# GroupNorm over 32 groups: the unrolled passes of VectorE and TensorE become small loops with the buffer number in a register

## Chip, cores and metric

The kernel runs on one NeuronCore of a Trainium2 chip; nothing else is placed on the chip by it. The metric is the device time of one execution in microseconds (us). The kernel before takes 633.19 us, the median of three runs (632.77 to 633.47).

## What is computed

The input is a bfloat16 tensor of 128 samples, 1024 channels and 32 x 16 points. Each sample's channels are split into 32 groups of 32; a group's 16384 values are brought to mean 0 and variance 1, and each channel is then scaled and shifted.

```python
G = 32
B, C, H, W = x.shape            # 128, 1024, 32, 16, bfloat16
xr = x.reshape(B, G, C // G, H, W)
mu = xr.mean(axis=(2, 3, 4), keepdims=True)
var = ((xr - mu) ** 2).mean(axis=(2, 3, 4), keepdims=True)
xn = (xr - mu) / jnp.sqrt(var + 1e-5)
return xn.reshape(B, C, H, W) * g[None, :, None, None] + b[None, :, None, None]
```

## The kernel before

A tile holds four samples: partition p carries one (sample, group) pair, and along the partition lie that group's 32 channels of 512 points, 32 KB. There are 32 tiles of 4 MB, each loaded once and stored once, and six buffers `xt[0..5]` in SBUF that tiles use in turn (tile i uses buffer (i + 4) mod 6).

Four engines handle each tile in a chain:

- **SyncE** (`sync_program`) issues every transfer, on one queue, in an order written out in the code. The first six loads go out at once. Then for each tile it waits for VectorE's count `s_dve` and issues the store (L171). After the stores of tiles 1, 4, 7, ... 25 it issues the next loads (two after tile 1, otherwise three; L163); each first waits until the store that empties its buffer has landed. Behind the six first loads and behind each run of loads it issues one *spacer* (L157), a load of 64 bytes a partition into a tile that nobody reads. There are ten of these.
- **TensorE** (`tensor_program`) waits for the load (L192) and sums the tile along the partition: 32 matmuls of 512 columns with the identity as weights, all added up in one PSUM bank `pa[j]` (L194). All 32 stand in the program for each of the six buffers.
- **VectorE** (`vector_program`) reduces the 512 columns of that bank to the negative mean (`mean`, L211). This mean of tile j+1 stands in the program ahead of the scaling of tile j.
- **ScalarE** (`scalar_program`) sums (x - mean) squared over the tile in two halves (L316), then makes the standard deviation with two small operations (L330, L337).
- **VectorE** then takes the reciprocal (L223), makes 32 scales and 32 shifts per partition (L226, L233), and runs 32 instructions of 512 points, one per channel, in place over the tile (L243). The last one raises `s_dve`.

VectorE, TensorE and ScalarE each run a counted loop (`loop`), a trip of which handles six tiles: the body is the six steps written out, every address a constant. It is split in two parts (`first`: buffers 0 to 3, `second`: 4 and 5) and entered at the second, because 32 tiles are not a multiple of six. For VectorE and TensorE the option `ahead` puts the set-up code behind the loop body. At the end of a trip each engine lowers the semaphores that it counts with (`settle` and `counts`), which costs VectorE three semaphore instructions, one register addition and a branch every six tiles.

## Time and profile before

| | |
|---|---|
| median of three runs | 633.19 us |
| profiled execution, its own time | 633.13 us |
| its span, first to last instruction | 631.3 us |
| busy: ScalarE | 476.2 us (75%) |
| busy: VectorE | 375.8 us (60%) |
| busy: TensorE matmul | 255.1 us (40%) |
| transfers: 32 loads, 32 stores of 4096 KB, 10 spacers of 8 KB | 268.57 MB, mean 425 GB/s |
| mean granted TensorE clock | 0.73 |

The profile's times are of the one profiled execution. The span runs from the first to the last instruction, and the execution's own time is 1.83 us longer. "Busy" counts engine work only; register, branch and semaphore instructions are not in it. The queue of an engine name with a q (SPq) stands for its issuing of transfers. "PEq L192" as a releaser is TensorE's wait for a load.

### The profile page before, as it was taken

To read this page: it belongs to the slowest core of one execution; us is meant where nothing else is said; L and a number is where in the kernel's file an instruction comes from. 1 tells how busy PE (TensorE), PEld (TensorE's weight loads), DVE (VectorE), ACT (ScalarE), POOL (GpSimd) and SP (SyncE) were. 2 spreads that over 40 slices of the span, in tenths; PEclk is the share of its full clock that TensorE was granted. 3 is DMA by queue.
4 is the path that set the end of the run, shared out by engine and by line. 5 is a ranking of instruction groups with operands and counts; after the bars stand their busy time and mean duration, and the time that the engine had idled before them with its cause. 6 is when DMAs were issued, how large, how long until landed. Compare 5 with 4: busy or idle time off the path is not lost. (4 is left out here: it accounts for less than half of the span.)

```text
span 631.3 us, 3704 instructions
## 1 busy us (share of the span) xinstructions
PE 255.1 (40%) x1009; PEld 105.4 (17%) x1025; DVE 375.8 (60%) x1188; ACT 476.2 (75%) x194; POOL 0.9 (0%) x7
## 2 busy tenths in 40 slices
PE   0967409009602750582087018404720770095000
PEld 0423103003201320230032003101300230032000
DVE  0057777774772777077727735770777177447771
ACT  0499999995994699189929965993899199649930
POOL 0000000000000000000000000000000000000000
PEclk9998858658855985687578659855975796598555
DMA  8999999999999999999999999999999999999996
GB/s 363 432 432 414 434 432 432 438 432 432 430 432 434 430 430 434 432 430 432 432 432 432 432 432 430 432 432 432 430 432 434 432 430 432 432 432 436 438 394 283
DMA packets 10756, 268.57 MB, mean 425 GB/s; under 512 B 2560, under 2 KB 2560, under 8 KB 2560
## 3 DMA queue, kind: packets, MB, share of 16 engines
q1 hardware_dynamic: 10656, 268.52, 99.0%
q10 hardware_dynamic: 96, 0.00, 0.0%
q14 instruction: 3, 0.02, 0.0%
q8 instruction: 1, 0.02, 0.0%
HBM read 134.30 MB, written 134.22 MB: 425 GB/s over the span
## 5 line engine op out<-in xcount | busy, mean ns | idle before, releaser
L316 ACT ACTIVATE ja<-xt,negmean 128x8192 fp8e5<-128x8192 bf16 x64 | 455.5, 7117 | 126.9 <-DVE jd L211 125.5
L194 PE MATMUL pa<-xt,eye 128*128 128x512 bf16 x1008 | 254.9, 414 | 312.4 <-PEq L192 310.9
L243 DVE TENSOR_SCALAR xt<-xt,scl,bia 128x512 bf16<-128x512 bf16 x1024 | 333.7, 408 | 1.2
L194 PEld LDWEIGHTS pa<-xt,eye 128*128 128x128 bf16 x1024 | 105.3, 105 | 461.6 <-issue 366.0
L211 DVE TENSOR_SCALAR_CACHE_REDUCE jd<-pa 128x512 bf16<-128x512 f32 x33 | 22.7, 687 | 147.3 <-PE pa L194 145.4
L223 DVE RECIPROCAL rstd<-std 128x1 f32<-128x1 f32 x32 | 5.2, 163 | 78.1 <-ACT std L337 78.1
L316 ACT ACTIVATION_READ_ACCUMULATOR ja<-xt,negmean 128x1 f32 x64 | 11.9, 186 | 0.0
L337 ACT ACTIVATE std<-sq,half 128x1 f32<-128x1 f32 x32 | 9.4, 295 | 1.0
L330 ACT ACTIVATE half<-sq,eps_t 128x1 f32<-128x1 f32 x32 | 8.9, 278 | 0.0
L233 DVE SCALAR_TENSOR_TENSOR bia<-scl,negmean,gb 128x32 f32<-128x32 f32 x32 | 8.1, 252 | 1.1
L226 DVE TENSOR_SCALAR scl<-gb,rstd 128x32 f32<-128x32 f32 x32 | 7.7, 241 | 1.1
L262 DVE COPY gb<-gb_p 128x64 f32<-128x64 f32 x1 | 0.2, 226 | 10.7 <-PE gb_p L181 10.7
L181 PE MATMUL gb_p<-gb_b,rep 32*128 32x64 bf16 x1 | 0.2, 231 | 12.5 <-DMA gb_b<-in_b_dram 12.5
L211 DVE DVE_READ_ACCUMULATOR jd<-pa 128x1 f32 x33 | 2.7, 83 | 0.0
L312 ACT ACT_TABLE_LOAD x1 | 1.3, 1283 | 1.9 <-issue 1.9
L181 PEld LDWEIGHTS gb_p<-gb_b,rep 32*128 32x128 bf16 x1 | 0.1, 100 | 12.5 <-DMA gb_b<-in_b_dram 12.5
L261 DVE MEMSET ones_b<- 128x128 bf16 x1 | 0.2, 165 | 1.9 <-issue 1.9
L289 POOL TENSOR_SCALAR_AFFINE_SELECT rep<-ones_b 32x128 bf16<-32x128 bf16 x1 | 0.3, 303 | 0.0
L280 POOL TENSOR_SCALAR_AFFINE_SELECT eye<-ones_b 128x128 bf16<-128x128 bf16 x1 | 0.3, 294 | 1.7 <-DVE ones_b L261 1.7
L312 ACT ACTIVATE warm<-eps_t 128x1 f32<-128x1 f32 x1 | 0.2, 203 | 0.0
L298 POOL TENSOR_SCALAR eps_t<-ones_b 128x1 f32<-128x1 bf16 x1 | 0.2, 205 | 0.0
L378 POOL MEMSET const-uint8-127<- 128x1 uint8 x1 | 0.1, 103 | 0.0
(3 smaller groups left out, 0.3 us busy)
## 6 DMA issues: line engine op xcount, KB each, us to landing
xt<-in_x_dram SPq DMA_DIRECT2D x32, 4096.0 KB, 29.1
out_dram<-xt SPq DMA_DIRECT2D x32, 4096.0 KB, 33.2
spare<-in_x_dram SPq DMA_DIRECT2D x10, 8.0 KB, 29.2
gb_b<-in_g_dram ACTq DMA_DIRECT2D x1, 2.0 KB, 7.8
gb_b<-in_b_dram ACTq DMA_DIRECT2D x1, 2.0 KB, 11.0
```

The costliest lines, as they stand in the source:

```text
L181: pe.matmul(out=gb_p[:].rearrange("p a k -> p (a k)"), lhsT=rep[:], rhs=gb_b[:].rearrange("q a k -> q (a k)"), start=True, stop=True,).the ...
L194: m = pe.matmul(out=pa[j][:], lhsT=eye[:], rhs=xt[j][:, k * MM_FREE : (k + 1) * MM_FREE], start=(k == 0), stop=(k == NMM - 1),)
L211: dve.tensor_scalar(out=jd[j % 2][:], in0=pa[j % NBUF][:], scalar1=-inv_n, scalar2=None, op0=ALU.mult, op1=ALU.add, accum_out=col(negmean, j),
L223: dve.reciprocal(out=col(rstd, j), in_=col(std, j))._wait_ge(s_std, j + 1).then_inc(s_dd, 1)
L226: dve.tensor_scalar(out=scl[j][:], in0=gam, scalar1=col(rstd, j), scalar2=None, op0=ALU.mult,)._wait_ge(s_dd, 3 * j + 2).then_inc(s_dd, 1)
L233: dve.scalar_tensor_tensor(out=bia[j][:], in0=scl[j][:], scalar=col(negmean, j), in1=bet, op0=ALU.mult, op1=ALU.add,)._wait_ge(s_dd, 3 * j ...
L243: m = dve.tensor_scalar(out=span, in0=span, scalar1=scl[j][:, k : k + 1], scalar2=bia[j][:, k : k + 1], op0=ALU.mult, op1=ALU.add,)
L280: pool.affine_select(out=eye[:], in_=ones_b[:], pattern=[[-1, P]], compare_op=ALU.is_equal, fill=0.0, base=0, channel_multiplier=1,)._wait ...
L312: act.activation(out=warm[:], in_=eps_t[:], func=ACT.Sqrt)
L316: m = act.activation(out=ja[:], in_=xt[j][:, h * F // 2 : (h + 1) * F // 2], func=ACT.Square, bias=col(negmean, j), scale=1.0, accum_out=s ...
L330: act.activation(out=col(half, j), in_=sq[:, 2 * j : 2 * j + 1], func=ACT.Identity, bias=eps_t[:], scale=inv_n,)._wait_ge(s_sq, 3 * j + 1) ...
L337: act.activation(out=col(std, j), in_=sq[:, 2 * j + 1 : 2 * j + 2], func=ACT.Sqrt, bias=col(half, j), scale=inv_n,)._wait_ge(s_sq, 3 * j + ...
```

## The change

- **VectorE.** The six written-out steps become one outer loop over the 32 tiles (`nc.Fori`); the buffer number `j` is in a register, and the addresses of the mean, the deviation and the tile are worked out from it by register instructions. The 32 scaling instructions become an inner loop of four rounds of eight (`SCALE_STEP`), with the channel number in a register too. The built program has, for each scaling instruction, two fused register instructions ahead of it, one with six register operations and one with two, and each round ends with a register addition and a compare-and-branch. The scales, shifts and reciprocal have one buffer instead of six. Waits go against constants, and a semaphore is lowered right after each wait. After the last round a `drain` comes ahead of the raise of `s_dve`.
- **TensorE.** Of a tile's 32 matmuls the first and the last stand alone; the 30 between run as ten rounds of three (`MM_STEP`), the column offset worked out from the round's register. A round of the built program has three fused register instructions (six, five and five operations), two plain register additions, three matmuls and a compare-and-branch.
- **SyncE.** The ten spacers and their waits are gone. Loads, stores and their order stay.
- **ScalarE** does what it did. `loop` loses `ahead`; GpSimd's set-up code is only wrapped in a function.

```diff
+MM_STEP = 3
+SCALE_STEP = 8
...
-    xt = [sb.tile([P, F], BF16, name=f"xt{j}") for j in range(NBUF)]
+    x_all = sb.tile([P, NBUF * F], BF16, name="x_all")
+    xt = [x_all[:, j * F : (j + 1) * F] for j in range(NBUF)]
...
         for i in range(min(NBUF, NT)):
             load(i)
-        spacer()
         for i in range(NT):
...
                 for n in range(max(NBUF, i + 1 + NBUF - RUN), min(i + 1 + NBUF, NT)):
                     load(n)
-                spacer()
...
         def step(j):
             pe.wait_ge(ld[j], 16)
             pe.sem_inc(ld[j], -16)
-            for k in range(NMM):
-                m = pe.matmul(
-                    out=pa[j][:],
-                    lhsT=eye[:],
-                    rhs=xt[j][:, k * MM_FREE : (k + 1) * MM_FREE],
-                    start=(k == 0),
-                    stop=(k == NMM - 1),
+            def add(rhs, start=False, stop=False):
+                return pe.matmul(
+                    out=pa[j][:], lhsT=eye[:], rhs=rhs, start=start, stop=stop
                 )
-            m.then_inc(s_pe, 1)
+            add(xt[j][:, 0:MM_FREE], start=True)
+            with nc.Fori(0, (NMM - 2) // MM_STEP, 1, ...) as r:
+                for n in range(MM_STEP):
+                    add(xt[j][:, bass.ds((r * MM_STEP + n + 1) * MM_FREE, MM_FREE)])
+            add(xt[j][:, F - MM_FREE : F], stop=True).then_inc(s_pe, 1)
...
+        with nc.Fori(ENTRY, NT + ENTRY, 1, engines=es) as i:
+            j = i % NBUF
+            mean((i + 1) % NBUF)
+            dve.reciprocal(out=rstd[:], in_=at(std, j, 1))._wait_ge(s_std, 1).then_inc(
+                s_dd, 1
+            )
+            dve.sem_inc(s_std, -1)
...
+            dve.wait_ge(s_dd, 3)
+            dve.sem_inc(s_dd, -3)
-            for k in range(KC):
-                span = xt[j][:, k * HW : (k + 1) * HW]
-                m = dve.tensor_scalar(
-                    out=span,
-                    in0=span,
-                    scalar1=scl[j][:, k : k + 1],
-                    scalar2=bia[j][:, k : k + 1],
-                    op0=ALU.mult,
-                    op1=ALU.add,
-                )
...
-            m.then_inc(s_dve, 1)
+            with nc.Fori(0, KC // SCALE_STEP, 1, engines=es) as r:
+                for n in range(SCALE_STEP):
+                    k = r * SCALE_STEP + n
+                    span = at(x_all, j * KC + k, HW)
+                    dve.tensor_scalar(
+                        out=span,
+                        in0=span,
+                        scalar1=at(scl, k, 1),
+                        scalar2=at(bia, k, 1),
+                        op0=ALU.mult,
+                        op1=ALU.add,
+                    )
+            dve.drain()
+            dve.sem_inc(s_dve, 1)
```

`at(t, j, n)` is `t[:, bass.ds(j * n, n)]`, a slice whose start is in a register.

More of the change, by code (lines that the diff above doesn't have):

```diff
@@ L20 @@
 MM_FREE = 512
+MM_STEP = 3
+SCALE_STEP = 8
 ENTRY = 4
-SPARE = 32
 @with_exitstack
@@ L47 @@
     TRIPS = (NT + ENTRY) // NBUF
-    assert F % MM_FREE == 0 and NT + ENTRY == TRIPS * NBUF
+    assert KC % SCALE_STEP == 0 and F % MM_FREE == 0 and (NMM - 2) % MM_STEP == 0
+    assert NT + ENTRY == TRIPS * NBUF
     x_v = x.rearrange("(t n) (g k) h w -> t (n g) (k h w)", n=NS, g=G)
@@ L64 @@
     warm = sb.tile([P, 1], F32, name="warm")
-    spare = sb.tile([P, SPARE], BF16, name="spare")
     ones_b = sb.tile([P, P], BF16, name="ones_b")
@@ L72 @@
     std = sb.tile([P, NBUF], F32, name="std")
-    rstd = sb.tile([P, NBUF], F32, name="rstd")
-    scl = [sb.tile([P, KC], F32, name=f"scl{j}") for j in range(NBUF)]
-    bia = [sb.tile([P, KC], F32, name=f"bia{j}") for j in range(NBUF)]
-    pa = [ps.tile([P, MM_FREE], F32, name=f"pa{j}") for j in range(NBUF)]
+    rstd = sb.tile([P, 1], F32, name="rstd")
+    scl = sb.tile([P, KC], F32, name="scl")
+    bia = sb.tile([P, KC], F32, name="bia")
+    pa_all = ps.tile([P, NBUF * MM_FREE], F32, name="pa_all")
+    pa = [pa_all[:, j * MM_FREE : (j + 1) * MM_FREE] for j in range(NBUF)]
     gb_p = ps.tile([P, 2, KC], F32, name="gb_p")
@@ L85 @@
     s_pe, s_mean, s_sq, s_std = sem("s_pe"), sem("s_mean"), sem("s_sq"), sem("s_std")
-    s_spare = sem("s_spare")
     s_dd, s_dve = sem("s_dd"), sem("s_dve")
+    s_gbp = sem("s_gbp")
     def buf(i):
@@ L93, in col, with loop @@
         return t[:, j % NBUF : j % NBUF + 1]
-    def loop(engine, prepare, step, settle, counts, ahead=False):
+    def loop(engine, prepare, step, settle, counts):
         es = bass.OrderedEngineSet([engine.engine])
-        name = f"trip_{engine.engine.name}"
-        first, middle, over, second, leave, past, begin, end = (
-            f"{name}_{part}"
-            for part in "first middle over second leave past begin end".split()
-        )
-        trip = nc.alloc_registers(f"{name}_n", engines=es)
-        def set_up():
-            prepare()
-            for s, _, n in counts:
-                if n:
-                    engine.sem_inc(s, n)
-            nc.regs_mov(trip, 0)
-            nc.br(second, engines=es)
-        if ahead:
-            nc.regs_mov(trip, -1)
-            nc.br_lt(trip, -1, on_true=first, on_false=middle, engines=es)
-        else:
-            set_up()
+        first, second, end = (
+            f"trip_{engine.engine.name}_{part}" for part in ("first", "second", "end")
+        )
+        trip = nc.alloc_registers(f"trip_{engine.engine.name}", engines=es)
+        prepare()
+        for s, _, n in counts:
+            engine.sem_inc(s, n)
+        nc.regs_mov(trip, 0)
+        nc.br(second, engines=es)
         with nc.body(first, valid_engines=es):
@@ L124, in loop @@
                 step(j)
-            nc.br(middle if ahead else second, engines=es)
-        if ahead:
-            with nc.body(middle, valid_engines=es):
-                nc.br_lt(trip, 0, on_true=over, on_false=second, engines=es)
+            nc.br(second, engines=es)
         with nc.body(second, valid_engines=es):
@@ L135, in loop @@
             nc.regs_alu(trip, trip, 1, op=ALU.add)
-            nc.br_lt(trip, TRIPS, on_true=first, on_false=leave, engines=es)
-        with nc.body(leave, valid_engines=es):
-            nc.br(past if ahead else end, engines=es)
-        if ahead:
-            with nc.body(over, valid_engines=es):
-                nc.br(past, engines=es)
-            with nc.body(past, valid_engines=es):
-                nc.br_lt(trip, TRIPS, on_true=begin, on_false=end, engines=es)
-            with nc.body(begin, valid_engines=es):
-                set_up()
+            nc.br_lt(trip, TRIPS, on_true=first, on_false=end, engines=es)
         nc.switch_bb(end)
-    spacers = [0]
     def sync_program(sync):
-        def spacer():
-            n = spacers[0]
-            spacers[0] += 1
-            if n:
-                sync.wait_ge(s_spare, 16 * n)
-            sync.dma_start(out=spare[:], in_=x_v[0][:, 0:SPARE]).then_inc(s_spare, 16)
         def load(i):
@@ L186, in prepare @@
                 stop=True,
-            ).then_inc(s_pe, 1)
+            ).then_inc(s_gbp, 1)
             pe.wait_ge(s_eye, 1)
@@ L192, in step @@
             pe.sem_inc(ld[j], -16)
-            for k in range(NMM):
-                m = pe.matmul(
-                    out=pa[j][:],
-                    lhsT=eye[:],
-                    rhs=xt[j][:, k * MM_FREE : (k + 1) * MM_FREE],
-                    start=(k == 0),
-                    stop=(k == NMM - 1),
-                )
-            m.then_inc(s_pe, 1)
-        loop(pe, prepare, step, lambda: None, [], ahead=True)
+            def add(rhs, start=False, stop=False):
+                return pe.matmul(
+                    out=pa[j][:], lhsT=eye[:], rhs=rhs, start=start, stop=stop
+                )
+            add(xt[j][:, 0:MM_FREE], start=True)
+            with nc.Fori(
+                0,
+                (NMM - 2) // MM_STEP,
+                1,
+                engines=bass.OrderedEngineSet([pe.engine]),
+            ) as r:
+                for n in range(MM_STEP):
+                    add(xt[j][:, bass.ds((r * MM_STEP + n + 1) * MM_FREE, MM_FREE)])
+            add(xt[j][:, F - MM_FREE : F], stop=True).then_inc(s_pe, 1)
+        loop(pe, prepare, step, lambda: None, [])
         pe.drain()
@@ L207, in vector_program, with at, mean @@
     def vector_program(dve):
+        es = bass.OrderedEngineSet([dve.engine])
         gam, bet = gb[:, 0, :], gb[:, 1, :]
-        def mean(j):
+        def at(t, j, n):
+            return t[:, bass.ds(j * n, n)]
+        def mean(j, n=0):
             dve.tensor_scalar(
-                out=jd[j % 2][:],
-                in0=pa[j % NBUF][:],
+                out=jd[n][:],
+                in0=at(pa_all, j, MM_FREE),
                 scalar1=-inv_n,
@@ L217, in mean @@
                 op1=ALU.add,
-                accum_out=col(negmean, j),
-            )._wait_ge(s_pe, j + 2).then_inc(s_mean, 1)
-        def step(j):
-            mean(j + 1)
-            dve.reciprocal(out=col(rstd, j), in_=col(std, j))._wait_ge(
-                s_std, j + 1
-            ).then_inc(s_dd, 1)
+                accum_out=at(negmean, j, 1),
+            )._wait_ge(s_pe, 1).then_inc(s_mean, 1)
+            dve.sem_inc(s_pe, -1)
+        dve.memset(ones_b[:], 1.0).then_inc(s_set, 1)
+        dve.tensor_copy(out=gb[:], in_=gb_p[:])._wait_ge(s_gbp, 1).then_inc(s_dd, 1)
+        dve.wait_ge(s_dd, 1)
+        dve.sem_inc(s_dd, -1)
+        mean(ENTRY, 1)
+        with nc.Fori(ENTRY, NT + ENTRY, 1, engines=es) as i:
[5 more added lines that the diff above has]
+            dve.sem_inc(s_std, -1)
             dve.tensor_scalar(
-                out=scl[j][:],
+                out=scl[:],
                 in0=gam,
-                scalar1=col(rstd, j),
+                scalar1=rstd[:],
                 scalar2=None,
                 op0=ALU.mult,
-            )._wait_ge(s_dd, 3 * j + 2).then_inc(s_dd, 1)
+            )._wait_ge(s_dd, 1).then_inc(s_dd, 1)
             dve.scalar_tensor_tensor(
-                out=bia[j][:],
-                in0=scl[j][:],
-                scalar=col(negmean, j),
+                out=bia[:],
+                in0=scl[:],
+                scalar=at(negmean, j, 1),
                 in1=bet,
@@ L239, in step @@
                 op1=ALU.add,
-            )._wait_ge(s_dd, 3 * j + 3).then_inc(s_dd, 1)
-            for k in range(KC):
-                span = xt[j][:, k * HW : (k + 1) * HW]
-                m = dve.tensor_scalar(
-                    out=span,
-                    in0=span,
-                    scalar1=scl[j][:, k : k + 1],
-                    scalar2=bia[j][:, k : k + 1],
-                    op0=ALU.mult,
-                    op1=ALU.add,
-                )
-                if k == 0:
-                    m._wait_ge(s_dd, 3 * j + 4)
-                if k == KC - 2 and j == NBUF - 1:
-                    m.then_inc(s_dd, 1)
@@ L255, in step @@
-            m.then_inc(s_dve, 1)
-        def settle():
-            dve.wait_ge(s_dd, 3 * NBUF + 2)
-        def prepare():
-            dve.memset(ones_b[:], 1.0).then_inc(s_set, 1)
-            dve.tensor_copy(out=gb[:], in_=gb_p[:])._wait_ge(s_pe, 1).then_inc(s_dd, 1)
-            dve.sem_inc(s_pe, ENTRY)
-            mean(ENTRY)
-        loop(
-            dve,
-            prepare,
-            step,
-            settle,
-            [
-                (s_pe, NBUF, 0),
-                (s_std, NBUF, ENTRY),
-                (s_dd, 3 * NBUF + 1, 3 * ENTRY),
-            ],
-            ahead=True,
-        )
@@ L279, in pool_program @@
-    def pool_program(pool):
-        pool.affine_select(
-            out=eye[:],
-            in_=ones_b[:],
-            pattern=[[-1, P]],
-            compare_op=ALU.is_equal,
-            fill=0.0,
-            base=0,
-            channel_multiplier=1,
-        )._wait_ge(s_set, 1).then_inc(s_eye, 1)
-        pool.affine_select(
-            out=rep[:].rearrange("q (n a) -> q n a", n=NS),
-            in_=ones_b[0:G, :].rearrange("q (n a) -> q n a", n=NS),
-            pattern=[[0, NS], [-1, G]],
-            compare_op=ALU.is_equal,
-            fill=0.0,
-            base=0,
-            channel_multiplier=1,
-        ).then_inc(s_rep, 1)
-        pool.tensor_scalar(
-            out=eps_t[:],
-            in0=ones_b[:, 0:1],
-            scalar1=EPS,
-            scalar2=None,
-            op0=ALU.mult,
-        ).then_inc(s_set, 1)
+            )._wait_ge(s_dd, 2).then_inc(s_dd, 1)
@@ new lines, in vector_program, with pool_program @@
+            dve.drain()
+            dve.sem_inc(s_dve, 1)
+    def pool_program(pool):
+        def prepare():
+            pool.affine_select(
+                out=eye[:],
+                in_=ones_b[:],
+                pattern=[[-1, P]],
+                compare_op=ALU.is_equal,
+                fill=0.0,
+                base=0,
+                channel_multiplier=1,
+            )._wait_ge(s_set, 1).then_inc(s_eye, 1)
+            pool.affine_select(
+                out=rep[:].rearrange("q (n a) -> q n a", n=NS),
+                in_=ones_b[0:G, :].rearrange("q (n a) -> q n a", n=NS),
+                pattern=[[0, NS], [-1, G]],
+                compare_op=ALU.is_equal,
+                fill=0.0,
+                base=0,
+                channel_multiplier=1,
+            ).then_inc(s_rep, 1)
+            pool.tensor_scalar(
+                out=eps_t[:],
+                in0=ones_b[:, 0:1],
+                scalar1=EPS,
+                scalar2=None,
+                op0=ALU.mult,
+            ).then_inc(s_set, 1)
+        prepare()
@@ L359 @@
             block.scalar(scalar_program)
-        nc.sync.wait_ge(s_spare, 16 * spacers[0])
         for j in range(NBUF):
```

## The prediction

> **What bounds the kernel now.** The page's overview comes first: which engine or queue is full, and where.

> ```profile
> span 631.3 us, 3704 instructions
> ...
> DMA  8999999999999999999999999999999999999996
> ...
> q1 hardware_dynamic: 10656, 268.52, 99.0%
> ```

> The queue of SyncE is full from the second slice to the last but one. The records of single transfers say how full: a 32 KB descriptor takes 1.218 us in the mean, each of the 16 DMA engines has 64 x 8 = 512 of them, which makes 623.6 us. The first starts 2.0 us after the span's start, and the last ends 2.0 us before its end. So some 4 us of 627.3 are lost, nearly all in the last 15 us, where some engines have finished before others. A change can gain very little here. It can lose whatever makes this queue run dry, so I next read how far ahead of the queue each transfer is issued.

> ```profile
> 51.21 15.22 SPq L171 DMA_DIRECT2D out_dram<-xt  x2
> 74.36 10.02 SPq L163 DMA_DIRECT2D xt<-in_x_dram  x2
> 84.42 0.43 SPq L157 DMA_DIRECT2D spare<-in_x_dram  x1
> 84.90 26.55 SPq L171 DMA_DIRECT2D out_dram<-xt  x3
> 113.18 19.65 SPq L163 DMA_DIRECT2D xt<-in_x_dram  x3
> 542.84 74.80 SPq L171 DMA_DIRECT2D out_dram<-xt  x6
> ```

> These are SyncE's issues in order of time. Beside each I put the start of its first descriptor. The difference is its *cover*, the time by which it may be late at no cost. Store 0 (51.21): 10.6 us; store 1 (66.09): 5.4; store 4 (111.12): 8.9; later the third store of each three 13 to 15; the last three stores 7.7, 2.5 and 0.8. Cover is thin in the first 110 us, ample in the middle, and gone at the end.

> What sets those issues is the chain of waits, and the groups give its prices.

> ```profile
> 553.47 7.12 PE pa L194 x28
> 561.35 7.23 ACT ja L316 x2
> 606.09 0.17 DVE rstd L223
> 606.85 10.43 DVE xt L243 x32
> ```
> ```profile
> L316 ACT ACTIVATE ja<-xt,negmean 128x8192 fp8e5<-128x8192 bf16 x64 | 455.5, 7117 | 126.9 <-DVE jd L211 125.5
> L243 DVE TENSOR_SCALAR xt<-xt,scl,bia 128x512 bf16<-128x512 bf16 x1024 | 333.7, 408 | 1.2
> ```

> The chain that ended last goes load 29, TensorE, mean, ScalarE for tiles 29, 30 and 31, one scaling pass, store. ScalarE's step is 14.86 us a tile (std 576.03, then 590.89). A tile's transfers need 2 x 9.75 = 19.5 us, so no engine is the bound in throughput; only latency at the two ends is.

> **VectorE's scaling.** Now 32 instructions start 323 ns apart, 10.43 us a pass. The change puts two fused register instructions ahead of each, and a register addition and a branch behind each eight. No fused one is in this trace. What is there, in the records of control instructions at the end of a trip (not counted as busy): three semaphore instructions at 65.773, 65.872, 65.965, an addition at 66.060, a branch at 66.151, the next mean at 66.493. A slot is 95 ns, and a branch costs 342 ns until the engine works again.

> ```profile
> 66.49 0.69 DVE L211 TENSOR_SCALAR_CACHE_REDUCE jd<-pa 128x512 bf16<-128x512 f32 x1 [0.43 <-issue]
> ```

> That 0.43 us, idle for no releaser, is the same stretch in the timeline. Lower bound: a fused instruction costs one slot like any other, a scaling instruction another; 8 x 3 x 95 + 91 + 342 = 2.71 us a round against 2.58 of engine work, 10.9 us a pass. Upper bound: each of the eight operations costs a slot of its own; 8 x 9 x 95 + 433 = 7.27, 29 us a pass. In between: an addition's record is 40 ns and a semaphore instruction's 21, so the operation itself is at most some 19 ns, which gives 8 x (285 + 6 x 19) + 433 = 3.63 and 14.5 us. A fused instruction exists to share the decoding, so I stay near the low end: 10 ns for an operation beyond the first, 8 x 345 + 433 = 3.19, **12.8 us a pass (+2.4)**. The slots do not hide behind the engine any more, because they are longer than its 323 ns.

> [...]

> **Around the pass.** From the reciprocal to the first scaling instruction now 0.76 us (591.22 to 591.98). Added: a wait, a semaphore, a register move and a scaling slot at 95 each, a branch 342, fused instructions 145 and 105: 0.97, so 1.75 us **(+1.0)**. Ahead of a mean: addition 91, branch 342, fused 145 and 105, a slot 95: 0.8 us, where it was 0.03 to 0.43. With the mean's 0.77 VectorE's step is 12.8 + 1.75 + 0.77 + 0.8 = **16.1 us a tile**, longer than ScalarE's 14.86: in every run of tiles in a row VectorE now sets the pace. The semaphores lowered after the waits on `s_pe` and `s_std` lie beside the mean and the reciprocal (0.69 and 0.16 us against 0.095). The `drain` waits for work that the raise of `s_dve` waited for anyway.

> **TensorE.** A tile now takes 9.2 us with the clock low at first (15.00 to 24.21), 7.07 in a run. A round's slots by its records: a slot 76 ns (semaphore to weight load), a branch 208 plus a slot. Three fused at 126, 116, 116; two additions 152; three matmuls with weights 3 x 108 (76 + 32); branch 284: 1.12 us against 0.65 of array time. Ten rounds and 0.6 for the rest make **11.8 us (+2.6 for tile 0, +3.0 for tile 29, which took 8.8)**. Bounds: no extra for operations beyond the first, a matmul in one slot, 0.89 a round, 9.5 us; 7.1, the array's own pace; above, every operation a slot, 20 us.

> **Spacers.** Loads and stores start 9.69 us apart; across a spacer it is 9.74 (149.01 to 158.75). Ten of them give back 0.5 us where the queue is full; SyncE's 0.43 us for each is hidden by the cover behind it. The boundary without a spacer that the trace shows, store to load, loses nothing (119.96 to 129.65). The boundary of load and store whose spacer had been issued 47 us earlier lost 0.84 (51.25 to 61.79). If that is what a load followed at once by a store costs, nine more cost 7.6 us. I take the nearer row, -0.5.

> **The sum.** At the start: store 0 comes 2.6 + 1.0 + 2.4 = 6.0 us later, inside its 10.6. Store 1 comes a step later, 57.2 + 16.1 = 73.3 against 66.1: 7.2 late, 5.4 covered, the queue idles 1.8. Store 4 comes at 57.2 + 4 x 16.1 = 121.6, 10.5 late; 1.8 is already lost and 8.9 covered: nothing. In the middle a third store is later by 3.0 + 3.4 + 2 x 1.24 = 8.9, under 13: hidden. At the end: loads are later by 1.8 - 0.5 = 1.3; TensorE +3.0; tile 29's deviation to its store +3.4; tiles 30 and 31 +1.24 each, because VectorE's step is now the longer; less 0.9, for the last store waited that long on slow DMA engines, which will then be free. 1.3 + 3.0 + 3.4 + 2.5 - 0.9 = +9.3. The profiled execution took 633.13 us, 0.06 under the median, which I leave out: **642 us**.

> **The rivals.** A measurement of this kernel tells some 0.2% from no change, which is 631.9 to 634.5.

> *VectorE's register work hides.* At one slot for a fused instruction a step is 10.9 + 3.3 = 14.2, under ScalarE's 14.86, and TensorE takes 9.5. Then store 1 is covered, and the end is later by about 0.5 + 1.0 + 0.7 - 0.5 - 0.9: 634. For it: the slots nearly equal the engine's 323 ns. Against: eight operations would have to be free. Chance 0.2, 0.13 of it within 0.2%.

> *The queue gains.* Without spacers, boundaries lose neither 0.05 us each nor the 0.84, and VectorE and TensorE hide: 633.1 - 1.4 = 631.7. It needs the whole of the first rival as well, and the last store has under 1 us of cover. 0.03.

> *TensorE's clock stays low.* With gaps in every round it may stay at the 427 ns between matmuls that the first ten of tile 0 show, against 216 after: 32 x 0.427 = 13.7 us a tile. Store 1 is another 1.9 late with no cover, and tile 29 too: 646; with 14.5 us a pass it is a step of 17.8: store 1 is 7 us beyond its cover, store 4 another 5, the end 15: about 660. Together with passes of 13 to 14.5, chance 0.15. [...]

> *VectorE becomes the bound in throughput.* From 16.2 us a pass a step is over 19.5 us, the transfers' pace. With 40 ns an operation (the addition's record) a pass is 4 x (8 x 525 + 433) = 18.5, a step 21.8: 62.9 for store 0, 31 x 21.8, and 14 from the last issue to the end: 754. Against: it takes the whole record for the shared part too. 0.1.

> **How the numbers follow.** My case, passes of 11.2 to 14 us and TensorE at 10 to 13, gives 635 to 655 and has 0.52. Below it lies the hidden case from 634 up; above it the low clock to 662. The range 634 to 662 leaves out the throughput case, the gain, and a part of the hidden one: 2 in 10. Faster 0.03, within 0.2% 0.13, slower 0.84.

> **What would show it.** In the profile after: L243's successor (now L232) with starts near 390 to 400 ns apart and idle time "issue" ahead of it, step 16 us; matmuls in threes, 11 to 12 us a tile; the queue dry for 2 us near 70 us and in the last 30; the second store issued near 73 us. Scaling starts still 323 ns apart would make it wrong at once, and so would idle stretches of the queue at every boundary of load and store.

## The result, and the profile after

The kernel after takes **639.33 us**, the median of six runs (638.81 to 639.61); the kernel before takes 633.18 us in six runs on the same chip. The ratio is 1.0097, with a 95% interval of 1.0084 to 1.0110. The change makes the kernel slower by 6.2 us. The profiled execution after took 639.09 us, with a span of 637.1.

The page after, its overview of the span, the transfer share and rate in 40 slices, and the row of SyncE's queue:

```profile
span 637.1 us, 8220 instructions
...
DMA  8999999999999999999999999999999999999966
GB/s 362 432 448 403 428 430 438 432 436 432 428 428 436 436 432 432 434 422 432 432 436 432 432 432 428 432 438 436 430 430 426 428 438 438 432 422 430 414 278 268
...
q1 hardware_dynamic: 9216, 268.44, 98.1%
```

The same rate row of the kernel before:

```profile
GB/s 363 432 432 414 434 432 432 438 432 432 430 432 434 430 430 434 432 430 432 432 432 432 432 432 430 432 432 432 430 432 434 432 430 432 432 432 436 438 394 283
```

The queue is still full from the second slice on, with no dry place in the middle. The difference is the last three slices: 414, 278, 268 GB/s where there were 438, 394, 283. The instructions have more than doubled, 3704 to 8220, and nearly all of the new ones are register work and branches.

SyncE's issues in order of time (start, length, queue, line, transfer, count):

```profile
51.87 15.18 SPq L138 DMA_DIRECT2D out_dram<-x_all  x2
...
546.47 77.90 SPq L138 DMA_DIRECT2D out_dram<-x_all  x6
```

Store 0 goes at 51.87 (before 51.21), store 1 at 66.70 (before 66.09): 0.6 us later, inside its cover of 5.4. The last store goes at 624.04 (before 617.30). So the start costs nothing and the end costs 6.74 us.

The end in the timeline (start, busy us, engine, line, operation, count, idle time before and its releaser), tile 29's sums and mean, then the reciprocals and scaling rounds of tiles 30 and 31:

```profile
555.90 19.40 PE L161 MATMUL pa_all<-x_all,eye 128*128 128x512 bf16 x64 [30.02 <-PEq L158]
565.55 0.69 DVE L188 TENSOR_SCALAR_CACHE_REDUCE jd<-pa_all 128x512 bf16 x1 [15.74 <-PE pa_all L161]
...
596.17 0.17 DVE L207 RECIPROCAL rstd<-std 128x1 f32 x1 [0.56 <-ACT std L304]
...
611.04 0.16 DVE L207 RECIPROCAL rstd<-std 128x1 f32 x1 [0.56 <-ACT std L304]
...
612.33 2.75 DVE L232 TENSOR_SCALAR x_all<-x_all,scl,bia  x8 [0.56 <-DVEq L227]
615.31 2.74 DVE L232 TENSOR_SCALAR x_all<-x_all,scl,bia  x8 [0.24 <-issue]
...
621.25 2.74 DVE L232 TENSOR_SCALAR x_all<-x_all,scl,bia  x8 [0.23 <-issue]
```

The start of tile 29 and its mean in the kernel before:

```profile
551.81 1.44 PE L194 MATMUL pa<-xt,eye 128*128 128x512 bf16 x3 [31.78 <-PEq L192]
560.61 0.69 DVE L211 TENSOR_SCALAR_CACHE_REDUCE jd<-pa 128x512 bf16<-128x512 f32 x1 [16.54 <-PE pa L194]
```

Set against the chain of before, step by step:

| step | before | after | change |
|---|---|---|---|
| TensorE starts tile 29 | 551.81 | 555.90 | **+4.09** |
| from there to the mean | 8.80 | 9.65 | +0.85 |
| mean to tile 31's reciprocal | 45.48 | 45.49 | +0.01 |
| reciprocal to first scaling | 0.76 | 1.29 | +0.53 |
| scaling pass and store issue | 10.45 | 11.71 | +1.26 |
| last store to the span's end | 14.00 | 13.06 | -0.94 |
| sum (span) | 631.3 | 637.1 | +5.80 |

The step between two reciprocals is 596.17 to 611.04, 14.87 us, as before: VectorE still waits 0.56 us for the deviation each time, so ScalarE still sets the pace. The two loops cost 2.6 us on the path, of which 0.94 came back at the end. The largest term is one that the prediction did not have: tile 29 starts 4.1 us late, although its load was issued in good time and its first descriptor ran at 536.93 (before 537.11).

The records of single transfers show why. A transfer has 16 completions, as many as the page counts DMA engines, and where the queue is full 16 packets are in flight at once (in 94% of the time from 20 to 600 us before, 96% after). The completions of load 29, in us, in order:

| | first | 12th | 13th | 14th | 15th | last |
|---|---|---|---|---|---|---|
| before | 546.6 | 547.1 | 549.8 | 551.1 | 551.1 | 551.7 |
| after | 546.4 | 547.8 | 548.2 | 548.3 | 548.8 | **555.8** |

The tile waits for the slowest: TensorE starts it 0.1 us behind the last completion in either kernel, at 551.81 and at 555.90. In the kernel after, the last completion comes 7 us behind the fifteenth. The packets in flight show the same ahead of the last store: after, from 619.91 to 624.65 us there is one at a time; before, from 614.62 to 617.34 there are mostly four. So after the change one DMA engine is late. (The trace does not name the engine of a completion or of a packet; that one engine stands behind the packets that run alone is read from their number.) The gap between first and last completion grows through the whole run, from 0.4 us at 13 us to 2.9 at 169, 6.9 at 401 and 10.5 at 595; in the kernel before it is 2.0, 3.0, 4.3 and 5.1 at those times.

### The profile page after: what moved, and what is told of

Same layout as the page of the kernel before. It is cut to its first block, busy times and chain, and to the rows that moved or that the text cites. A ratio compares the mean times of both kernels' runs of the same rounds, so it can differ in the third digit from the quotient of the medians.

```text
span 637.1 us, 8220 instructions
## 1 busy us (share of the span) xinstructions
PE 284.6 (45%) x1025; PEld 103.2 (16%) x1025; DVE 394.9 (62%) x1188; ACT 476.4 (75%) x194; POOL 0.9 (0%) x7
## 3 DMA queue, kind: packets, MB, share of 16 engines
q1 hardware_dynamic: 9216, 268.44, 98.1%
## 5 line engine op out<-in xcount | busy, mean ns | idle before, releaser
L283 ACT ACTIVATE ja<-x_all,negmean 128x8192 fp8e5<-128x8192 bf16 x64 | 455.6, 7119 | 131.7 <-DVE jd L188 130.3
L161 PE MATMUL pa_all<-x_all,eye 128*128 (+1 forms) x1024 | 284.4, 402 | 289.7 <-PEq L158 266.7
L232 DVE TENSOR_SCALAR x_all<-x_all,scl,bia x1024 | 351.1, 413 | 40.0 <-issue 22.1
L161 PEld LDWEIGHTS pa_all<-x_all,eye 128*128 128x128 bf16 x1024 | 103.1, 101 | 470.7 <-issue 421.0
L188 DVE TENSOR_SCALAR_CACHE_REDUCE jd<-pa_all 128x512 bf16 (+1 forms) x33 | 22.8, 692 | 155.0 <-PE pa_all L161 140.5
L207 DVE RECIPROCAL rstd<-std 128x1 f32 x32 | 5.2, 163 | 21.0 <-ACT std L304 21.0
L283 ACT ACTIVATION_READ_ACCUMULATOR ja<-x_all,negmean 128x1 f32 x64 | 12.0, 187 | 0.0
L211 DVE TENSOR_SCALAR scl<-gb,rstd 128x32 f32<-128x32 f32 x32 | 7.7, 242 | 1.1
L188 DVE DVE_READ_ACCUMULATOR jd<-pa_all (+1 forms) x33 | 2.8, 84 | 0.0
```

The costliest lines, as they stand in the source:

```text
L161: return pe.matmul(out=pa[j][:], lhsT=eye[:], rhs=rhs, start=start, stop=stop)
L188: dve.tensor_scalar(out=jd[n][:], in0=at(pa_all, j, MM_FREE), scalar1=-inv_n, scalar2=None, op0=ALU.mult, op1=ALU.add, accum_out=at(negmea ...
L207: dve.reciprocal(out=rstd[:], in_=at(std, j, 1))._wait_ge(s_std, 1).then_inc(s_dd, 1)
L211: dve.tensor_scalar(out=scl[:], in0=gam, scalar1=rstd[:], scalar2=None, op0=ALU.mult,)._wait_ge(s_dd, 1).then_inc(s_dd, 1)
L232: dve.tensor_scalar(out=span, in0=span, scalar1=at(scl, k, 1), scalar2=at(bia, k, 1), op0=ALU.mult, op1=ALU.add,)
L283: m = act.activation(out=ja[:], in_=xt[j][:, h * F // 2 : (h + 1) * F // 2], func=ACT.Square, bias=col(negmean, j), scale=1.0, accum_out=s ...
```

## The experiments

What made one DMA engine late was open. The theories of the texts on record are these. A: the spacers had held the engines together. B: the looped engines' own work spreads them, the longer pass or the instructions in it. C: control instructions (register work, branches, semaphores) do it by their number, on whichever engine. D: VectorE's register instructions do it. E: the traffic of semaphores does it. "Spread" is the gap between the first and the last completion of one transfer, at its largest in a run unless a transfer is named. Beside each run the kernel before was timed again; its medians were 633.2 to 633.4.

**1. The loops with the spacers back.**

```diff
 kernel after
+        spacer()          # behind the first loads
...
+                spacer()  # behind each run of loads
```

> The changed kernel with the ten spacers put back, nothing else. Theory A (the end is late because the slowest of the 16 DMA engines falls behind the fastest when no spacer stands between loads and stores; loops in VectorE and TensorE cost only their own latency at the end): the spread of a transfer's completions stays near the 5.1 us of the kernel before instead of 9.4 to 10.5, load 29 is seen some 4 us earlier, and the time is 635 to 636. Theory B (the spread comes from what the looped engines do, the spacers are worth their own 0.5 us): spread 9 to 10 us, 639.3 to 640.

640.28 us, ratio 1.0115 [1.0100, 1.0131]. The spread of a transfer's completions reaches 11.0 us. TensorE's tile 29 and its mean in the timeline:

```profile
556.98 18.23 PE L175 MATMUL pa_all<-x_all,eye 128*128 128x512 bf16 x60 [30.05 <-PEq L172]
...
566.63 0.69 DVE L202 TENSOR_SCALAR_CACHE_REDUCE jd<-pa_all 128x512 bf16 x1 [15.33 <-PE pa_all L175]
```

The spacers do not bring the engines together again: 556.98 is 1.1 us later still. Theory A falls.

**2. The kernel before without the spacers.**

```diff
 kernel before
-        spacer()
...
-                spacer()
```

> The kernel before without its ten spacers, nothing else. Theory A: the spread grows by about 1 us a period as in the changed kernel, load 29 is seen some 4 us later, less the 0.9 us of cover and some 0.5 us that the spacers took: 636 to 637. Theory B: the spread stays at 5 us and the time is 632.5 to 633.

633.67 us, ratio 1.0007 [0.9998, 1.0016], no difference that can be told. The spread reaches 6.4 us (before 5.2), more than the 5 that theory B expected and far less than A's. With run 1 no gain or loss from the spacers can be told in either kernel.

**3. and 4. One loop at a time.** Run 3 is the kernel after with TensorE's 32 matmuls written out; run 4 is run 2 with TensorE's loop of three.

```diff
 run 3, kernel after
-            with nc.Fori(0, (NMM - 2) // MM_STEP, 1, ...) as r:
...
+            for k in range(NMM):
+                m = pe.matmul(...)
```

> The changed kernel with TensorE's 32 matmuls written out again: no spacers, VectorE in loops. By the traces TensorE's loop costs 9.65 against 8.8 us for tile 29, so both theories have 638.3 to 638.8, 0.6 to 0.9 below the changed kernel. Theory A has the spread at 9 to 10 us; theory B, if it is TensorE's register work that spreads the DMA engines, has 635 and a spread near 5.

> The kernel before without spacers and with TensorE's loop of three matmuls a round; VectorE as before, written out. VectorE's loop costs 1.8 us from the deviation to the store in the traces (11.2 against 13.0), so theory A has 637.3 to 637.8 with a spread of 9 to 10 us. Theory B, if it is VectorE's register work: 633.5 to 634 and a spread near 5.

Run 3: 637.48 us, 1.0076 [1.0062, 1.0089]; tile 29 starts at 554.40, the spread reaches 9.2. Run 4: 634.41 us, 1.0017 [1.0008, 1.0026]; it starts at 552.56, spread 6.9. VectorE's side does most of it. Neither time lies in a range that was written down (638.3 to 638.8 or 635; 637.3 to 637.8 or 633.5 to 634): both loops take a part. What of VectorE's side, its longer pass or its instructions, these two cannot say.

**5. An idle engine's control instructions.** GpSimd has no work after the set-up. Here it runs a loop of 550 rounds, eight semaphore instructions, an addition and a branch each, ending near 470 us. Nobody waits for that semaphore; VectorE and TensorE are those of before.

```diff
 kernel before, GpSimd behind its set-up
+        with nc.Fori(0, 550, 1, engines=es):
+            for _ in range(4):
+                pool.sem_inc(s_extra, 1)
+                pool.sem_inc(s_extra, -1)
```

> The kernel before, with GpSimd, which is idle there, running a loop of 550 rounds of eight semaphore instructions, an addition and a branch: some 5500 control instructions, where the changed kernel has some 4500 more than the kernel before. Nobody waits for it. Theory C (it is the number of control instructions that any sequencer runs, not what VectorE does with them, that slows one DMA engine during stores): spread of completions at the end 8 to 10 us against 5.1, 636 to 637. Theory D (it is VectorE's own register instructions or register addresses): spread near 5, 633 to 633.6.

**640.95 us**, 1.0119 [1.0103, 1.0134]: 7.5 us, more than the change itself, and above the 636 to 637 that theory C expected; the spread reaches 12.7. The page, and the queues of the transfer view:

```profile
span 639.0 us, 9221 instructions
...
DMA  8999999999999999999999999999999999999866
GB/s 359 431 444 407 431 443 433 425 427 427 443 433 433 423 431 437 439 431 425 427 431 443 431 431 429 425 443 435 427 429 427 439 441 429 427 427 433 369 281 269
...
q1 hardware_dynamic: 10656, 268.52, 97.9%
...
q14 instruction: 3, 0.02, 0.0%
```

Its timeline at tile 29, and its group of scaling instructions:

```profile
558.94 16.34 PE L195 MATMUL pa<-xt,eye 128*128 128x512 bf16 x62 [30.44 <-PEq L193]
```
```profile
L244 DVE TENSOR_SCALAR xt<-xt,scl,bia 128x512 bf16<-128x512 bf16 x1024 | 333.7, 413 | 1.2
```

The tail is that of the kernel after, 369, 281, 269 GB/s, with VectorE's pass untouched (idle 1.2 us in all, as before). Load 29's first fifteen completions lie between 546.5 and 551.5 us, the last at 558.8: again one engine. The transfers carry the same bytes, and the instruction transfers (q14) are the same three packets as before, so no fetching of code is behind it. Neither VectorE nor TensorE is needed for the effect: control instructions make it, on an engine that nobody waits for. So theory D falls as the only cause. The run also shows when. GpSimd's last branch is at 470.5 us. From 13 to 469 us the spread grows from 1.6 to 11.7 us (before: 2.0 to 4.6), and in the 126 us after that by only 1.0 more (before: 0.5). So most of the growth falls in the time in which the loop runs.

**6. Half of the fused instructions.** The kernel after with the 32 scaling instructions written out. The channel is then a constant, and only the buffer stays in a register: one fused instruction instead of two for each, no inner branch.

```diff
 kernel after
-            with nc.Fori(0, KC // SCALE_STEP, 1, engines=es) as r:
-                for n in range(SCALE_STEP):
...
+            for k in range(KC):
...
-                        scalar1=at(scl, k, 1),
+                    scalar1=scl[:, k : k + 1],
```

> The changed kernel with the 32 scaling instructions of a tile written out: buffer still in a register, channel a constant, so that one fused register instruction of a few operations stands ahead of each instead of two, and no branch. Scaling starts go back to the engine's 323 ns, a pass to 10.4 us instead of 11.85. Theories C and D both: some 36 control instructions fewer a tile, about half of VectorE's extra ones, so half of the extra spread: 7 to 8 us at the end instead of 10. Time 635 to 637, of which 1.4 us from the shorter pass and some 2 from the spread. If the spread stays at 10: 637.5 to 638.

636.61 us, 1.0045 [1.0031, 1.0059]. Its page, and its group of scaling instructions:

```profile
span 634.8 us, 6908 instructions
```
```profile
L230 DVE TENSOR_SCALAR x_all<-x_all,scl,bia x1024 | 333.7, 413 | 8.2 <-DVEq L227 8.2
```

The 22.1 us of idle time "issue" are gone and the pass is 10.43 us again: one fused instruction hides behind a scaling instruction. But tile 29 still starts at 554.43, 2.6 us later than before, with spread 9.0, where 7 to 8 was expected. A pass at its old length does not cure the late engine.

**7. A semaphore instruction beside each scaling instruction.** The kernel before with 1024 more control instructions on VectorE.

```diff
 kernel before, in step
             for k in range(KC):
+                dve.sem_inc(s_extra, 1 if k % 2 == 0 else -1)
```

> The kernel before with one semaphore instruction behind each scaling instruction, on a semaphore that nobody waits for; a slot of 95 ns, so the 323 ns between scaling starts hide it and VectorE's times stay. 32 more control instructions a tile. Theories C and D (number of instructions): spread at the end 6.5 to 7.5 instead of 5.1, 634.2 to 635. If only register addresses matter: 633 to 633.6, spread 5.

651.57 us, 1.0283 [1.0269, 1.0297]: a miss, and no test of what control instructions do, because it changed a second thing. The page and the transfer view:

```profile
span 650.2 us, 4744 instructions
```
```profile
q14 instruction: 29, 0.24, 0.1%
```

Instead of three packets of code there are 29, and 27 of them, 8 KB and some 0.31 us each, lie between 10 and 615 us, about five in each trip. VectorE's body of six tiles was some 233 instructions (1243 records in 5.3 trips) and is now some 425. Why the packets come with the longer body, no run shows. VectorE waited longer too:

```profile
DVE jd L211 <- issue: 17.6, 3, 6.2
```

Ahead of its means it stood idle 17.6 us for no releaser that the profile shows, up to 6.2 us at a time; in the kernel before it was 2.0 us in all. Load 29's fifteenth completion is at 555.3, its last at 569.6. What of the 18 us belongs to the packets, and what to the 1024 instructions, this run cannot say.

**8. Register instructions only, at half the number.** GpSimd runs 1375 rounds of an addition and a branch, no semaphores.

```diff
 kernel before, GpSimd behind its set-up
+        with nc.Fori(0, 1375, 1, engines=es):
+            pass
```

> The kernel before, with GpSimd running 1375 rounds of a register addition and a branch, no semaphore and no memory: 2750 control instructions, half of e5's. Theory C (the number of control instructions, of whatever kind and engine): half of e5's effect, spread of completions 8 to 9.5 us against 5.1 and 12.7, 636 to 637.5. Theory E (in e5 it was the traffic of semaphores): spread near 5, 633 to 633.6, and the changed kernel's cause would be open again.

635.78 us, 1.0036 [1.0022, 1.0050]. The page and the transfer view:

```profile
span 634.0 us, 6471 instructions
```
```profile
GB/s 362 430 433 418 430 432 433 430 430 430 429 434 432 431 440 434 430 433 432 430 430 431 430 434 431 436 436 436 431 432 430 432 429 432 432 428 434 442 337 269
```

Instructions that touch no semaphore do it too: 337, 269 at the end where there were 394, 283. Tile 29 starts at 553.89, 2.1 us late, for 2750 instructions; run 5 had twice as many and 7.1 us. So the price is not simply in proportion: an instruction of run 5's mix weighs 1.7 times as much, or the price grows faster than the number. Theory C had expected 636 to 637.5 and a spread of 8 to 9.5, theory E 633 to 633.6 and 5; measured are 635.8 and 7.6. E falls, and C holds in direction, but not in its proportion.

**9. Neither inner loop.** The kernel after with matmuls and scaling instructions written out, the buffer still in VectorE's register: the edits of runs 3 and 6 together.

> The changed kernel with the scaling instructions and the matmuls of a tile both written out; what is left of the change is the buffer in VectorE's register and the missing spacers. If the parts add up: 639.33 less 1.9 for the matmul loop (the scaling-loop kernel) and 2.7 for the channels (the kernel with channels written out): 634.7. Theory C by its count of instructions (some 5000, between 3704 and 6302): spread 7 to 8 us, and 634.5 to 635.5.

634.82 us, 1.0022 [1.0013, 1.0031], span 632.9; tile 29 starts at 552.70, spread 7.3. With runs 3 and 6 and the kernel after, this is a square:

| | matmuls written out | matmuls in threes |
|---|---|---|
| channels written out | 634.82 (run 9) | 636.61 (run 6) |
| channels in eights | 637.48 (run 3) | 639.33 (after) |

The scaling loop costs 2.7 us in either column and TensorE's loop 1.8 in either row; with the 1.6 from the kernel before to run 9 that is the whole. None of these versions beats the kernel before.

All kernels but run 7, by where the slowest engine stands at load 29:

| kernel | instructions | first completion | last completion | last store | median us |
|---|---|---|---|---|---|
| before | 3704 | 546.6 | 551.7 | 617.30 | 633.2 |
| run 2 | 3694 | 546.1 | 552.1 | 617.55 | 633.7 |
| run 4 | 5342 | 546.2 | 552.4 | 619.23 | 634.4 |
| run 9 | 5006 | 546.0 | 552.6 | 618.38 | 634.8 |
| run 8 | 6471 | 546.7 | 553.8 | 619.89 | 635.8 |
| run 3 | 6302 | 546.1 | 554.3 | 621.34 | 637.5 |
| run 6 | 6908 | 546.2 | 554.3 | 621.03 | 636.6 |
| after | 8220 | 546.4 | 555.8 | 624.04 | 639.3 |
| run 1 | 8230 | 546.8 | 556.8 | 625.11 | 640.3 |
| run 5 | 9221 | 546.5 | 558.8 | 625.48 | 641.0 |

The first completion stays between 546.0 and 546.8. The last one moves with the number of instructions, about 1.3 us per thousand from the first row to the last, though not evenly: run 4 has 1650 more than run 2 and only 0.3 us, while the same loop adds 1.7 us between runs 9 and 6. These are single executions.

## Why the prediction was right and where it was not

Direction and range held; the sum came near (642 against 639.3) because terms that were too large stood where a missing one belonged. That is luck: of what was to show the mechanism, only the idle time "issue" ahead of the scaling instructions and drier last slices came, the latter for another reason. Scaling starts near 390 ns, a step of 16 us, 11 to 12 us for a tile on TensorE and store 1 near 73 us did not.

**VectorE's pass: right in mechanism, too large.** It forecast rounds of 3.19 us, a pass of 12.8 (+2.4). The waits and the groups of the kernel after:

```profile
DVE x_all L232 <- issue: 22.1, 96, 0.2
DVE rstd L207 <- ACT std L304: 21.0, 24, 5.4
DVE x_all L232 <- DVEq L227: 17.9, 32, 0.6
```
```profile
L232 DVE TENSOR_SCALAR x_all<-x_all,scl,bia x1024 | 351.1, 413 | 40.0 <-issue 22.1
```

The 96 waits of 0.23 us are the three round boundaries of 32 passes. A round is 2.97 us, so four are 11.9; on the path the pass added 1.23. Within a round scaling instructions start 332 ns apart (345 forecast). The parts were further off than their sum: a fused instruction of six operations takes a slot of 211 ns (145 forecast), one of two 100 (105), the scaling instruction's own slot 22 (95). The forecast's 10 ns for an operation beyond the first was chosen between bounds without a row of a fused instruction; by 211 and 100 it is some 28 ns. Six operations in one fused instruction still take less than six plain additions would, 211 ns against 432 (an estimate, from the addition's slot of 72 ns in the same rounds). That it is the decoding that they share, the reason given for the low price, no run shows. Of the 0.22 us by which a round was too long, 0.10 lie in the eight steps and 0.12 in the round's end: 2.97 less 8 x 332 leaves 0.31 us, where 0.43 was taken from the branch at the end of a trip. From the record of a round's branch to the next instruction's it is some 190 ns where the branch is taken and 84 at the end of a pass, where it is not.

**Ahead of the pass: half of the forecast.** Reciprocal to first scaling was to be 1.75 us (+1.0); it is 1.29 (+0.53). Of the 17.9 us before L227 each pass has 0.56.

**VectorE sets the pace: wrong.** The step was to be 16.1 us against ScalarE's 14.86. It is 14.87 less the wait of 0.56, 14.3, and ScalarE still sets the pace. So the +2.5 for tiles 30 and 31 and the 1.8 us of dry queue after store 1 did not come: store 1 went at 66.70, not 73.3. This was the condition of the first rival, that VectorE's register work hides under ScalarE's step, and here that rival was right. Its time of 634 was not reached for the reason below.

**TensorE: too large.** The group of matmuls:

```profile
L161 PE MATMUL pa_all<-x_all,eye 128*128 (+1 forms) x1024 | 284.4, 402 | 289.7 <-PEq L158 266.7
```

A round was to be 1.12 us and is 0.90 to 0.94. The fused instructions were priced about right: 137, 113 and 113 ns until the next instruction, against 126, 116 and 116. The term that was too large is the three matmuls with their weight loads: 324 ns were forecast, and in a round of 0.90 us they take some 112 of the sequencer's time. Tile 29, with the clock low at first (0.5 granted until 559.6 us, matmuls 427 ns apart), takes 9.65 us, +0.85 where +3.0 was forecast. The clock did not stay low, though every round has a gap of about 0.3 us: matmuls of a round are 216 ns apart while 1.0 is granted, and the mean granted clock is 0.754, above the 0.729 of before. Short gaps stood in the trace before too, single ones, of 0.50 us here and 0.68 ahead of another tile, and both tiles ran at the full pace of 7.07 us:

```profile
24.72 7.07 PE L194 MATMUL pa<-xt,eye 128*128 128x512 bf16 x32 [0.50 <-PEq L192]
```

**Spacers: -0.5 forecast, nothing found.** Run 2 against the kernel before is +0.5, inside what can be told; run 1 against the kernel after is +0.9. The rejected price of 0.84 us for each boundary would have cost 7.6 us and is ruled out by run 2.

**What was missed: +4.1 us on the way to tile 29.** The prediction read the 99.0% of the queue and the last 15 us, where "some engines have finished before others", and took that spread as fixed; it even booked 0.9 us back. It priced control instructions on their own engine only. Runs 5 and 8 show that on an engine off the path they also hold up a DMA engine (load 29's last completion at 558.8 and 553.8, before at 551.7). That those of VectorE and TensorE do the same in the kernel after is read from taking them out: its largest spread of 10.5 us falls to 9.2 in run 3, 9.0 in run 6 and 7.3 in run 9. By the measured terms without it, 0.85 + 0.53 + 1.26 - 0.94 = 1.7, the kernel would have been near 635 us, an estimate.

**What stays open.** Which step of an instruction delays the DMA engine is not known, nor which of the 16 it is. Every execution here was recorded instruction by instruction, so these runs cannot tell the instruction from the writing of its record.

## What to carry to other kernels

With the queue full (98.1 to 99.0%), tile 29 was there only when the last of its 16 completions had come, 5.1 us behind the first before (551.7 and 546.6) and 9.4 after (555.8 and 546.4), so compare the first and the last completion of a transfer and not only the queue's share. Count instructions on all engines, register work and semaphores too: some 5500 more on an engine with nothing else to do cost 7.5 us here, in executions that were all recorded. And when a loop body is made longer, look whether its code is fetched again during the run: run 7, with 27 such packets, paid 18 us for 1024 instructions that no one waited for.
